# Longer transfer rows and fixed homes in one arena, in a fused linear attention and Soft-MoE kernel

## The chip, the cores and the metric

The kernel runs on one core of a Trainium2 chip. The metric is the device time of one execution in microseconds (us), lower is better. The engines are TensorE (PE, with its weight loads as PEld), VectorE (DVE), ScalarE (ACT), GpSimd (POOL) and SyncE (SP), which here does nothing but issue DMA transfers.

## What is computed

Linear attention for 8 batches, 8 heads, 576 tokens and 64 dimensions a head, then a Soft-MoE layer over all 4608 tokens with 8 experts of 4 slots each. All of it is float32. Cut to what matters, the reference is:

```python
kv  = einsum('bhsd,bhse->bhde', k, v)
o   = einsum('bhsd,bhde->bhse', q, kv)
x   = o / sqrt(mean(o*o, -1) + 1e-6) * g_norm          # -> (4608, 512)
logits = x @ phi                                       # (4608, 32)
d   = exp(logits - logits.max(0)); d /= d.sum(0) + 1e-9
slots = d.T @ x                                        # 4 rows for each expert
y[e] = relu(slots[e] @ w1[e]) @ w2[e]                  # w1 512x1024, w2 1024x512
c   = exp(logits - logits.max(1)); c /= c.sum(1) + 1e-9
out = c @ y                                            # (4608, 512)
```

## The kernel before, in words

The 4608 tokens are worked in 36 token tiles (T = 0 to 35) of 128 tokens; four batches' pairs share nine tiles. The kernel has two passes, separated by the softmax over all tokens.

*Pass 1.* For each batch b, `Kv.products` (L159) and `Kv.borders` (L174) make k^T v on PE from a main part (512 of the 576 tokens, two halves g = 0, 1 of two head pairs each) and a border part (the other 64 tokens). `Kv.slots` turns that into a block matrix `bd` that gives the attention output and its product with phi in one go. `products(T)` (L227, and L218 for the tile that two batches share) makes token tile T from q and `bd`. ACT and DVE square, reduce and evict it, GpSimd scales it to x (`xts`, 14 buffers) and to parts of the logits. Every six tiles make a group with a running maximum, an exponential, and a sum of weighted x (`group_sum`, L361). The tables `first` and `kv_steps` set between which tiles the steps of batch b's kv stand: three tiles ahead of its first use, one step a tile; batch 1's two halves and borders are worked at T = 2.

*Pass 2.* `expert_h(e)` (L573) multiplies the slots by w1, `expert_y(e, hf)` (L591) by half hf of the columns of w2. Experts 0 to 3 run as they come. For experts 4 to 7 all `expert_h` come first, then all first halves, `mix(0)`, and then the output of the first half of the columns, with the second halves of w2 worked in between: the output is made in three chunks k of 12 token tiles and two parts f, so six calls of `output` for hf = 0 and six for hf = 1. Experts 4 and 5, second half, are worked after call 1, expert 6 after call 2, expert 7 after call 3, then `mix(1)` and the rest. `output` (L619) multiplies on PE, evicts one half with ACT (L627) and the other with DVE (L629), and stores 768 KB (L630).

*Transfers.* All are issued by SP, in one list, in order. An input or weight tile of 1 MB has 8 KB in each of 128 partitions; border tiles (`kvr`, `qr`) have 2 KB. The 1 MB tiles and the output stages share a ring of 17 slots (`ring`, `NSLOT`), the border tiles five slots (`rest`). Half of one expert's w1 goes into four border slots (`SPLIT`), another expert's w1 into x buffers that are no longer needed (`IN_X`), in eight transfers of 2 KB rows. Each transfer waits until the one that is eight places earlier in the list has landed, since they share a completion semaphore; where its slot had a reader, it waits for that too.

Of the kernel before, what the change touches and what calls it, by code (L numbers as in the profile page):

```python
# [8 lines left out]
F32 = mybir.dt.float32  # L9
# [5 lines left out]
P = 128  # L15
# [16 lines left out]
SLOT = 2048  # L32
NSLOT = 17
SPLIT = (4, 0)
IN_X = ((5, 0), (5, 1))
NREST = 5
# [5 lines left out]
def soft_moe_linear_attention(ctx: ExitStack, tc: tile.TileContext, kv_in, kvr_in, q_in, qr_in, w1_in, w2_in, c_in, out):  # L42
# [5 lines left out]
    ring = ctx.enter_context(tc.tile_pool(name="ring", bufs=NSLOT))  # L48
    rest = ctx.enter_context(tc.tile_pool(name="rest", bufs=NREST))
    wk = ctx.enter_context(tc.tile_pool(name="wk", bufs=2))  # L50


    kv_sb, kvr_sb, q_sb, qr_sb, w1_sb, w2_sb = {}, {}, {}, {}, {}, {}

    def load_kv(b):
        kvr_sb[b] = rest.tile([P, 512], F32, tag="rest", name=f"kvr{b}")
        for g in range(2):
            kv_sb[b, g] = ring.tile([P, SLOT], F32, tag="ring", name=f"kv{b}_{g}")
            nc.sync.dma_start(kv_sb[b, g], kv_in[b, g])
            if b == 0 and g == 0:  # L60
                nc.sync.dma_start(cst, c_in)
            if g == (b > 0):
                nc.sync.dma_start(kvr_sb[b], kvr_in[b])

    def load_q(b):
        if b % 2:
            qr_sb[b // 2] = rest.tile([P, 2, NPAIR, 64], F32, tag="rest", name=f"qr{b // 2}")
            nc.sync.dma_start(qr_sb[b // 2], qr_in[b // 2])
        q_sb[b] = ring.tile([P, NPAIR, 512], F32, tag="ring", name=f"q{b}")
        nc.sync.dma_start(q_sb[b], q_in[b])  # L70

    def load_w1(e):
        for k in range(2):
            if (e, k) == SPLIT or (e, k) in IN_X:

                if (e, k) == SPLIT:
                    parts = [rest.tile([P, 512], F32, tag="rest", name=f"w1_{e}_{k}_{i}") for i in range(4)]
                else:
                    T = NT - GROUPS[-1] - 8 + 4 * IN_X.index((e, k))
                    parts = [xts[(T + i) % NX].rearrange("p j n -> p (j n)")[:, :512] for i in range(4)]  # L80
                for i, t in enumerate(parts):
                    nc.sync.dma_start(t, w1_in[e, k, :, i // 2, i % 2 * 512 : i % 2 * 512 + 512])
                w1_sb[e, k] = [[parts[2 * c + j // 2][:, j % 2 * 256 : j % 2 * 256 + 256] for j in range(4)] for c in range(2)]
                continue
            t = ring.tile([P, 2, FF], F32, tag="ring", name=f"w1_{e}_{k}")
            nc.sync.dma_start(t, w1_in[e, k])
            w1_sb[e, k] = [[t[:, c, j * 256 : (j + 1) * 256] for j in range(4)] for c in range(2)]

    def load_w2(e, hf):
        w2_sb[e, hf] = ring.tile([P, 8, 256], F32, tag="ring", name=f"w2_{e}_{hf}")  # L90
        nc.sync.dma_start(w2_sb[e, hf], w2_in[e, hf])
# [5 lines left out]
    for b in range(B):  # L97
        load_kv(b)
        load_q(b)
# [24 lines left out]
    xts = []  # L124
    for i in range(NX):
        t = const.tile([P, 4, 129], F32, name=f"x{i}")
        nc.gpsimd.memset(t[:, :, 128:129], 1.0)
        xts.append(t)
# [13 lines left out]
    class Kv:  # L142
# [10 lines left out]
        def products(self, r):  # L153
            g, w = divmod(r, 2)
            main = kv_sb[self.b, g].rearrange("p (r w c n) -> p r w c n", r=2, w=2, c=4)
# [11 lines left out]
        def borders(self, gs):  # L167

            half = kvr_sb[self.b].rearrange("p (g w n) -> p g w n", g=2, w=2)
            for g in gs:  # L170
                for i in range(2):
                    for w in range(2):
                        lo, at = 64 * i, 64 * w
                        nc.tensor.matmul(  # L174
                            self.pkv[lo : lo + 64, w, g],
                            lhsT=half[at : at + 64, g, 1, lo : lo + 64],
                            rhs=half[at : at + 64, g, 0, lo : lo + 64],
                            start=False,
                            stop=g == gs[-1],
                        )  # L180
# [30 lines left out]
    def products(T):  # L211
# [3 lines left out]
        for r in range(NPAIR):  # L215
            if t == 4:
                for i in range(2):
                    nc.tensor.matmul(  # L218
                        o[64 * i : 64 * i + 64, r, :192],
                        lhsT=qr_sb[g][:, i, r],  # L220
# [4 lines left out]
            else:  # L225
                i, at = (0, t * P) if t < 4 else (1, (t - 5) * P)
                nc.tensor.matmul(  # L227
                    o[:, r, :192], lhsT=q_sb[2 * g + i][:, r, at : at + P], rhs=bds[i][:, r], start=True, stop=True
# [193 lines left out]
    for T in range(NT - 2):  # L422
# [38 lines left out]
        for _ in range(min(2, len(todo_sums))):  # L461
            group_sum(*todo_sums.pop(0))

# [26 lines left out]
    for i in todo_sums:  # L490
        group_sum(*i)
    fill(LATE_FILL[0], home=ps.tile([P, 512], F32, tag="m", name="fill"), cols=512)
# [38 lines left out]
    LATE = 4  # L531
    for e in range(NE - LATE):
        load_w1(e)
        load_w2(e, 0)
        load_w2(e, 1)
    for e in range(NE - LATE, NE):
        load_w1(e)
    for hf in range(2):
        for e in range(NE - LATE, NE):
            load_w2(e, hf)  # L540

# [25 lines left out]

    def expert_h(e):
        ph = ps.tile([P, 2, 512], F32, tag="m", name=f"ph{e}")[:, 0, :256]
        for c in range(4):  # L570
            w1 = w1_sb[e, c // 2]
            for j in range(4):
# [3 lines left out]
                    rhs=w1[c % 2][j],  # L576
# [10 lines left out]
    def expert_y(e, hf):  # L587
        w2 = w2_sb[e, hf]
        for c in range(8):
# [4 lines left out]
                rhs=w2[:, c],  # L594
# [120 lines left out]
```

## Time and profile before

| what | value |
|---|---|
| median of 3 runs | 177.37 us (177.13 to 177.51) |
| profiled execution: span from its first to its last instruction | 175.2 us |
| profiled execution: its own whole time | not listed; the span and what lies around it, about 2 us by the median |
| PE busy | 150.1 us (86%) |
| DVE, ACT, POOL busy | 88.7, 87.0, 56.0 us |
| DMA queue of SP, share of 16 engines' span | 98.3% |
| read from HBM, written to HBM | 61.93 MB, 9.44 MB |
| mean rate over the span | 407 GB/s |

All times of a view count from the start of the span. In the busy digits of 40 slices, a digit is the busy share in tenths (9 is 90% or more). A row of the order of time gives start and duration in us, engine, line, operation, output <- input and a count; in brackets stands how long the engine sat idle before and what ended it. "SPq" is SP's queue: its duration is that of issuing, not of the transfer. A row of the waits gives who waited <- for whom: us in total, times, the longest. A row of the DMA issues gives the count, KB each, and the median us from issue to landing. A row of a stretch gives start:end and length, then for PE, PEld, DVE, ACT and POOL the busy us and in parentheses the instructions, then the granted clock, the share of the DMA engines and GB/s.

### The profile page before, as it was taken

To read this page: it belongs to the slowest core of one execution; us is meant where nothing else is said; L and a number is where in the kernel's file an instruction comes from. 1 tells how busy PE (TensorE), PEld (TensorE's weight loads), DVE (VectorE), ACT (ScalarE), POOL (GpSimd) and SP (SyncE) were. 2 spreads that over 40 slices of the span, in tenths; PEclk is the share of its full clock that TensorE was granted. 3 is DMA by queue.
4 is the path that set the end of the run, shared out by engine and by line. 5 is a ranking of instruction groups with operands and counts; after the bars stand their busy time and mean duration, and the time that the engine had idled before them with its cause. 6 is when DMAs were issued, how large, how long until landed. Compare 5 with 4: busy or idle time off the path is not lost.

```text
span 175.2 us, 4888 instructions
## 1 busy us (share of the span) xinstructions
PE 150.1 (86%) x2033; PEld 108.3 (62%) x2033; DVE 88.7 (51%) x180; ACT 87.0 (50%) x224; POOL 56.0 (32%) x78
## 2 busy tenths in 40 slices
PE   7677999999989899999999869889979988989600
PEld 5456878899779788888986754556636533343200
DVE  1122155666466665557654679625886205357600
ACT  2116386878948957869777751102312203336400
POOL 7000156666556566364666465000000000000000
PEclk9999999999999999999999999999999999999975
DMA  5999999999999999999999999999999999999995
GB/s 185 413 428 414 424 424 427 422 419 421 428 419 424 419 419 424 423 426 417 436 419 423 432 426 420 413 395 369 415 423 428 421 428 423 419 420 415 425 426 209
DMA packets 12982, 71.69 MB, mean 409 GB/s; under 512 B 1440, under 2 KB 1568, under 8 KB 6176
## 3 DMA queue, kind: packets, MB, share of 16 engines
q1 hardware_dynamic: 12960, 71.37, 98.3%
q8 instruction: 16, 0.26, 0.5%
q14 instruction: 6, 0.05, 0.1%
HBM read 61.93 MB, written 9.44 MB: 407 GB/s over the span
## 4 chain that ended last, share of the span: by engine, by line
PE 39%; DMA 27%; DVE 12%; ACT 10%; issue 3%; POOL 2%; SPq 2%; POOLq 0%; DVEq 0%
PE o L227 17%; DMA w<-in_w_dram 16%; DMA kv<-in_kv_dram 8%; PE kvp_kv L159 8%; PE po L619 4%; DMA out_dram<-st 3%; DVE logits L304 3%; DVE st L629 3%; PE pS L361 2%; DVE ms L250 2%; POOL part L299 2%; ACT bd L194 2%; PE o L218 2%; ACT sq L237 2%; PE ph L573 2%
## 5 line engine op out<-in xcount | busy, mean ns | idle before, releaser
L227 PE MATMUL o<-bd,q 128*128 128x192 f32 x256 | 49.3, 336 | 1.5 <-ACT x L245 0.6
L227 PEld LDWEIGHTS o<-bd,q 128*128 128x128 f32 x256 | 40.8, 190 | 4.7 <-ACT x L245 1.6
L277 POOL TENSOR_TENSOR x<-x,r 128x512 f32<-128x512 f32 x34 | 34.7, 1042 | 0.0
L299 POOL TENSOR_TENSOR part<-part,r 128x512 f32<-128x512 f32 x17 | 17.8, 1048 | 50.7 <-DVE r L268 50.7
L304 DVE TENSOR_REDUCE logits<-part 128x64 f32<-128x512 f32 (+1 forms) x19 | 19.2, 1013 | 16.1 <-POOL part L299 16.0
L250 DVE TENSOR_REDUCE ms<-sq 128x16 f32<-128x1024 f32 (+1 forms) x19 | 22.0, 1157 | 6.3 <-ACT sq L237 6.3
L237 ACT ACTIVATE sq<-o 128x512 f32<-128x512 f32 x36 | 21.4, 596 | 6.6 <-PE o L227 6.1
L245 ACT COPY x<-o 128x512 f32<-128x512 f32 x34 | 20.7, 608 | 0.0
L159 PE MATMUL kvp_kv<-kv 128*64 128x64 f32 x480 | 17.3, 225 | 2.4 <-DMA kv<-in_kv_dram 2.4
L159 PEld LDWEIGHTS kvp_kv<-kv 128*64 128x64 f32 x480 | 15.2, 138 | 5.4 <-DMA kv<-in_kv_dram 3.1
L627 ACT COPY st<-po 128x768 f32<-128x768 f32 x12 | 9.4, 800 | 16.7 <-PE po L619 16.6
L591 PE MATMUL pY<-w,x 128*32 128x256 f32 x256 | 16.0, 382 | 1.2 <-DVE x L585 1.2
L629 DVE COPY st<-po 128x768 f32<-128x768 f32 x12 | 11.3, 956 | 7.9 <-PE po L619 5.9
L619 PE MATMUL po<-logits,z 32*128 32x384 f32 x96 | 13.8, 528 | 1.6 <-DVE st L629 0.6
L573 PE MATMUL ph<-w,sTe 128*32 128x256 f32 x224 | 13.0, 379 | 0.3 <-DVE sTe L514 0.3
L591 PEld LDWEIGHTS pY<-w,x 128*32 128x32 f32 x256 | 7.6, 109 | 8.3 <-DVE x L585 1.9
L244 ACT COPY part<-o 128x256 f32<-128x256 f32 x34 | 12.6, 371 | 0.0
L361 PE MATMUL pS<-x,d 128*32 128x129 f32 x288 | 10.7, 276 | 2.1 <-ACT d L349 2.1
L258 ACT ACTIVATE r<-ms,eps 128x16 f32<-128x16 f32 x17 | 5.2, 308 | 12.7 <-DVE ms L250 12.6
L619 PEld LDWEIGHTS po<-logits,z 32*128 32x128 f32 x96 | 5.5, 183 | 9.0 <-ACT st L627 3.6
L266 DVE SCALAR_TENSOR_TENSOR r<-ms,r 128x16 f32<-128x16 f32 x17 | 3.0, 176 | 14.9 <-ACT r L259 14.9
L573 PEld LDWEIGHTS ph<-w,sTe 128*32 128x32 f32 x224 | 7.2, 110 | 5.2 <-DVE sTe L514 0.6
(90 smaller groups left out, 146.7 us busy)
## 6 DMA issues: line engine op xcount, KB each, us to landing
w<-in_w_dram SPq DMA_DIRECT2D x29, 1024.0 KB, 19.1
kv<-in_kv_dram SPq DMA_DIRECT2D x16, 1024.0 KB, 14.3
out_dram<-st SPq DMA_DIRECT2D x12, 768.0 KB, 6.4
q<-in_qt_dram SPq DMA_DIRECT2D x8, 1024.0 KB, 14.2
kvr<-in_kr_dram SPq DMA_DIRECT2D x8, 256.0 KB, 14.9
x<-in_w_dram SPq DMA_DIRECT2D x8, 256.0 KB, 6.9
qr<-in_qr_dram SPq DMA_DIRECT2D x4, 256.0 KB, 14.1
w<-in_w_dram SPq DMA_DIRECT2D x4, 256.0 KB, 15.2
```

What stands on the lines that cost most here:

```text
L159: nc.tensor.matmul(self.pkv[lo : lo + 64, w, g], lhsT=main[:, w, 1, c, lo : lo + 64], rhs=main[:, w, 0, c, lo : lo + 64], start=c == 0 and ...
L227: nc.tensor.matmul(o[:, r, :192], lhsT=q_sb[2 * g + i][:, r, at : at + P], rhs=bds[i][:, r], start=True, stop=True)
L237: nc.scalar.activation(sqs[s][:, T - starts[s]], o[:, :, 32:160], AF.Square, scale=0.125)
L245: nc.scalar.copy(xts[T % NX][:, :, :128], o[:, :, 32:160])
L250: nc.vector.tensor_reduce(out=mss[s], in_=sqs.pop(s).rearrange("p t j (w d) -> p (t j w) d", w=2), axis=AX.X, op=ALU.add)
L277: nc.gpsimd.tensor_tensor(out=x, in0=x, in1=r[:, i].rearrange("p (j w) -> p j w", w=2).unsqueeze(3).to_broadcast([P, 4, 2, D]), op=ALU.mult,)
L299: engine.tensor_tensor(out=part, in0=part, in1=rs_of[s].unsqueeze(3).to_broadcast([P, STAGES[s], H, NS]), op=ALU.mult)
L304: nc.vector.tensor_reduce(out=L[:, pos(starts[s]) : pos(starts[s]) + STAGES[s]], in_=parts.pop(s).rearrange("p t h n -> p t n h"), axis=AX ...
L573: nc.tensor.matmul(ph[32 * j : 32 * j + 32], lhsT=sTe[:, (4 * e + c) * NS : (4 * e + c + 1) * NS], rhs=w1[c % 2][j], start=c == 0, stop=c ...
L591: nc.tensor.matmul(pY[32 * j : 32 * j + 32, hf, :256], lhsT=hTs[e][:, c], rhs=w2[:, c], start=e == 0 and c < 4, stop=e == NE - 1 and c >= 4,)
L619: nc.tensor.matmul(po[:, u, : CT * NS].rearrange("p (g x) -> p g x", g=2), lhsT=z[lo : lo + 32, f * P : (f + 1) * P], rhs=cT[k][lo : lo + 32],
L629: nc.vector.tensor_copy(out=st[:, 2:4], in_=po[:, :, : CT * NS])
```

## The change

*Layout.* kv and its border rows of a batch become one array with rows of 18 KB per partition (4608 numbers: for each half g 2048 main and 256 border numbers). The q of two batches and their shared border become one array with rows of 18 KB. A whole w1 of an expert has rows of 16 KB. A w2 has 16 KB too: for experts 0 to 3 both halves of the columns; for experts 4 to 7 unit 4 holds the first halves of experts 4 and 5, unit 5 those of 6 and 7, unit 6 the second halves of 4 and 5, unit 7 those of 6 and 7. The first loads are cut: kv of batches 0 and 1 in two rows of 9 KB each, the first two q arrays in 8 and 10 KB.

*Homes.* In place of the two rings there is one arena of 160 KB per partition. A table gives each load its home in it in units of 1 KB; a home is reused when the readers of what lay there are done. w1 of expert 5 goes into the x buffers (now one tile, `xall`, turned by six tiles), w1 of expert 6 into two pieces. 15 of 16 KB that GpSimd had as DMA scratch are taken for the arena.

*Stores.* Chunk k = 0 is stored as before in two transfers with rows of 6 KB; for k = 1 and 2 the two parts f go in one transfer with rows of 12 KB, issued once both are evicted.

The work of PE, ACT, DVE and GpSimd keeps its order. The core of the diff:

```diff
-SLOT = 2048
-NSLOT = 17
-SPLIT = (4, 0)
-IN_X = ((5, 0), (5, 1))
-NREST = 5
+TOK = 4608
+UNIT = 4096
+KB = 256
+ARENA = 160 * KB
+LATE = 4
+KV_AT = (0, 36, 54, 90, 108, 0, 18, 36)
+Q_AT = (18, 72, 142, 54)
+W_AT = {("w1", 0): (72,), ("w2", 0): (88,), ("w1", 1): (104,), ("w2", 1): (120,), ("w1", 2): (136,), ("w2", 2): (0,), ("w1", 3): (16,), ("w2", 3): (32,), ("w1", 4): (48,), ("w1", 5): None, ("w1", 6): (64, 152), ("w1", 7): (72,), ("w2", 4): (88,), ("w2", 5): (104,), ("w2", 6): (120,), ("w2", 7): (136,)}
+SCRATCH = 1024
...
+    def place(at, n):
+        return arena[:, at * KB : at * KB + n]
...
+    load_kv(0, 0)
+    nc.sync.dma_start(cst, c_in)
+    load_kv(0, 1)
+    load_q(0, 0)
+    load_kv(1, 0)
+    load_kv(1, 1)
+    load_q(0, 1)
+    load_kv(2)
...
+    loads_behind = {
+        9: lambda: (load_kv(5), load_kv(6), load_q(3), load_kv(7)),
+        18: lambda: [load_w(k, e) for e in range(2) for k in ("w1", "w2")],
+        27: lambda: (load_w("w1", 2), load_w("w2", 2), load_w("w1", 3)),
+        31: lambda: load_w("w2", 3),
+    }
...
-        st = ring.tile([P, 4, CT * NS], F32, tag="ring", name=f"st{hf}_{k}_{f}")
+        at = 6 * ((hf * NCH + k) * 2 + f)
+        st = place(at, 4 * CT * NS).rearrange("p (a n) -> p a n", a=4)
...
-        nc.sync.dma_start(out[hf, k, f], st)
+        if k == 0:
+            nc.sync.dma_start(out[hf, k, :, f], place(at, 4 * CT * NS))
+        elif f == 1:
+            nc.sync.dma_start(out[hf, k].rearrange("p f n -> p (f n)"), place(at - 6, 8 * CT * NS))
...
-    nc = bacc.Bacc("TRN2", target_bir_lowering=False, num_devices=1)
+    nc = bacc.Bacc("TRN2", target_bir_lowering=False, num_devices=1, dynamic_dma_scratch_size=SCRATCH)
```

The calls of `load_w` for the later weights stand among the work that frees their homes: w1 of experts 4 to 6 behind the last sums of x, w1 of expert 7 behind `expert_h(1)`, w2 units 4 and 5 behind `expert_y` of experts 0 and 1, units 6 and 7 behind that of expert 3.

Two places of SP's list show what moves. At its start the kernel before issues these; `kv_0` and `kv_1` are the halves of a batch, `kvr` its border rows, and the last number is of float32 per partition.

```order
L59 DMA kv_0_71<-in_kv_dram 128x2048
L61 DMA cst<-in_cs_dram 128x129
L63 DMA kvr_70<-in_kr_dram 128x512
L59 DMA kv_1_75<-in_kv_dram 128x2048
L70 DMA q_77<-in_qt_dram 128x2048
L59 DMA kv_0_80<-in_kv_dram 128x2048
L59 DMA kv_1_82<-in_kv_dram 128x2048
L63 DMA kvr_79<-in_kr_dram 128x512
L68 DMA qr_85<-in_qr_dram 128x512
L70 DMA q_87<-in_qt_dram 128x2048
```

The border rows of batch 1 (`kvr_79`) are a transfer of their own behind its second half. The changed kernel issues at the same place, with all of it in the arena:

```order
L66 DMA arena<-in_kv_dram 128x2304
L105 DMA cst<-in_cs_dram 128x129
L66 DMA arena<-in_kv_dram 128x2304
L70 DMA arena<-in_qt_dram 128x2048
L66 DMA arena<-in_kv_dram 128x2304 x2
L70 DMA arena<-in_qt_dram 128x2560
L66 DMA arena<-in_kv_dram 128x4608
```

Each half of batches 0 and 1 now carries its own border rows, and from batch 2 on a batch is one transfer. At the end of SP's list the kernel before has the last weights and, of its twelve stores, the six of hf = 0 as follows (the name gives k, then f):

```order
L91 DMA w_6_1_1609<-in_w_dram 128x2048
L91 DMA w_7_1_1611<-in_w_dram 128x2048
L630 DMA out_dram<-st_0_0_1921 128x1536
L630 DMA out_dram<-st_0_1_1931 128x1536
L630 DMA out_dram<-st_1_0_1957 128x1536
L630 DMA out_dram<-st_1_1_1975 128x1536
L630 DMA out_dram<-st_2_0_1999 128x1536
L630 DMA out_dram<-st_2_1_2009 128x1536
```

There each part is stored on its own. The changed kernel has at the end:

```order
L95 DMA arena<-in_w_dram 128x2048 x2
L95 DMA arena<-in_w_dram 128x4096 x5
L652 DMA out_dram<-arena 128x1536 x2
L654 DMA out_dram<-arena 128x3072 x2
L652 DMA out_dram<-arena 128x1536 x2
L654 DMA out_dram<-arena 128x3072 x2
```

Of each hf, stores 3 and 4 became one and stores 5 and 6 became one; the whole list has 42 transfers where there were 90.

More of the change, by code (lines that the diff above doesn't have):

```diff
@@ L41, in soft_moe_linear_attention @@
 @with_exitstack
-def soft_moe_linear_attention(ctx: ExitStack, tc: tile.TileContext, kv_in, kvr_in, q_in, qr_in, w1_in, w2_in, c_in, out):
+def soft_moe_linear_attention(ctx: ExitStack, tc: tile.TileContext, kv_in, q_in, w1_in, w2_in, c_in, out):
     nc = tc.nc
     const = ctx.enter_context(tc.tile_pool(name="const", bufs=1))
-    ring = ctx.enter_context(tc.tile_pool(name="ring", bufs=NSLOT))
-    rest = ctx.enter_context(tc.tile_pool(name="rest", bufs=NREST))
     wk = ctx.enter_context(tc.tile_pool(name="wk", bufs=2))
[L53 to L91, printed above, removed]
@@ L95, in soft_moe_linear_attention, with load_kv, load_q, kv_main @@
     g2 = cst[:, 128:129]
-    for b in range(B):
-        load_kv(b)
-        load_q(b)
+    arena = const.tile([P, ARENA], F32, name="arena")
+    xall = const.tile([P, NX, 4, 129], F32, name="xall")
+    xflat = xall.rearrange("p i j n -> p (i j n)")
+    def place(at, n):
+        return arena[:, at * KB : at * KB + n]
+    def load_kv(b, g=None):
+        lo, hi = (0, TOK) if g is None else (2304 * g, 2304 * g + 2304)
+        nc.sync.dma_start(place(KV_AT[b], TOK)[:, lo:hi], kv_in[b, :, lo:hi])
+    def load_q(g, half=None):
+        lo, hi = {None: (0, TOK), 0: (0, 2048), 1: (2048, TOK)}[half]
+        nc.sync.dma_start(place(Q_AT[g], TOK)[:, lo:hi], q_in[g, :, lo:hi])
+    def kv_main(b, g):
+        return place(KV_AT[b], TOK)[:, g * 2304 : g * 2304 + 2048]
+    def kv_rest(b, g):
+        return place(KV_AT[b], TOK)[:, g * 2304 + 2048 : g * 2304 + 2304]
+    def q_main(b):
+        return place(Q_AT[b // 2], TOK)[:, b % 2 * 2048 : b % 2 * 2048 + 2048].rearrange("p (r n) -> p r n", r=NPAIR)
+    def q_rest(g):
+        return place(Q_AT[g], TOK)[:, 4096:].rearrange("p (i r n) -> p i r n", i=2, r=NPAIR)
+    def homes(kind, u):
+        at = W_AT[kind, u]
+        if at is None:
+            return [xflat[:, :UNIT]]
+        return [place(a, UNIT // len(at)) for a in at]
+    def load_w(kind, u):
+        parts = homes(kind, u)
+        n = UNIT // len(parts)
+        for i, t in enumerate(parts):
+            nc.sync.dma_start(t, (w1_in if kind == "w1" else w2_in)[u, :, i * n : i * n + n])
+    def w_block(kind, u, i):
+        parts = homes(kind, u)
+        n = UNIT // len(parts)
+        k, at = divmod(i * 256, n)
+        return parts[k][:, at : at + 256]
+    load_kv(0, 0)
[6 more added lines that the diff above has]
+    load_kv(2)
+    load_q(1, 0)
+    load_kv(3)
+    load_q(1, 1)
+    load_kv(4)
+    load_q(2)
+    loads_behind = {
[4 more added lines that the diff above has]
+    }
     nc.scalar.preload_act_table_set("natural_log_exp_and_others")
@@ L123, in soft_moe_linear_attention @@
         nc.gpsimd.memset(bds[i], 0.0)
[L124 to L128, printed above, removed]
+    nc.gpsimd.memset(xall[:, :, :, 128:129], 1.0)
+    xts = [xall[:, (i + 6) % NX] for i in range(NX)]
     L = const.tile([P, NT + len(GROUPS) + 1, NS], F32, name="logits")
@@ L167, in borders @@
         def borders(self, gs):
-            half = kvr_sb[self.b].rearrange("p (g w n) -> p g w n", g=2, w=2)
             for g in gs:
+                half = kv_rest(self.b, g).rearrange("p (w n) -> p w n", w=2)
                 for i in range(2):
@@ L491, in soft_moe_linear_attention @@
         group_sum(*i)
+    for e in range(4, 7):
+        load_w("w1", e)
     fill(LATE_FILL[0], home=ps.tile([P, 512], F32, tag="m", name="fill"), cols=512)
@@ L701 @@
     arrays = {
-        "in_kv_dram": kv,
-        "in_kr_dram": kr,
+        "in_kv_dram": kv.reshape(B, P, TOK),
         "in_qt_dram": qm,
-        "in_qr_dram": qr,
         "in_w1_dram": np.ascontiguousarray(w1),
```

71 lines of the change are left out of this document (39 added, 32 removed).

## The prediction

> **What bounds the kernel now.** I read the profile's page first: the span, the busy digits and the DMA queues.
>
> ```profile
> span 175.2 us, 4888 instructions
> ...
> DMA  5999999999999999999999999999999999999995
> ...
> DMA packets 12982, 71.69 MB, mean 409 GB/s; under 512 B 1440, under 2 KB 1568, under 8 KB 6176
> ...
> q1 hardware_dynamic: 12960, 71.37, 98.3%
> ```
>
> The one queue of SP keeps the 16 DMA engines busy for 98.3% of the span. That looks like a kernel which ends when its bytes have been moved, so that whatever makes a byte cheaper makes it faster. The packets are the rows of the transfers and one mark per engine and transfer (90 transfers x 16 = 1440 under 512 B).
>
> Two things have to be asked before that is believed: who waits for a load, and what feeds the queue at the end. The waits by engine answer the first; only these rows name a load as what a compute engine on PE waited for.
>
> ```profile
> PEld kvp_kv L159 <- DMA kv<-in_kv_dram: 3.1, 3, 1.3
> PE kvp_kv L159 <- DMA kv<-in_kv_dram: 2.4, 3, 1.1
> PE kvp_o L159 <- DMA kv<-in_kv_dram: 1.0, 1, 1.0
> PEld pY L591 <- DMA w<-in_w_dram: 0.5, 1, 0.5
> ```
>
> The kv waits belong to the first batches, before 18 us, as PE's order of time shows:
>
> ```profile
> 15.61 1.15 PE L159 MATMUL kvp_kv<-kv 128*64 128x64 f32 x32 [0.49 <-DMA kv<-in_kv_dram]
> 17.91 1.15 PE L159 MATMUL kvp_kv<-kv 128*64 128x64 f32 x32 [1.15 <-DMA kv<-in_kv_dram]
> 18.99 0.46 PE L174 MATMUL kvp_kv<-kvr 64*64 64x64 f32 x16
> ```
>
> From there to the end the sum of load waits is 0.5 us: the arithmetic is a second chain, as long as the transfers, and loads run ahead of it. The second question is answered by the stores. These are issue times on SP (start, us) of stores 1, 5 and 6, and of the last:
>
> ```profile
> 147.25 0.35 SPq L630 DMA_DIRECT2D out_dram<-st  x1
> 156.73 0.33 SPq L630 DMA_DIRECT2D out_dram<-st  x1
> 158.48 1.20 SPq L630 DMA_DIRECT2D out_dram<-st  x2
> 166.06 0.35 SPq L630 DMA_DIRECT2D out_dram<-st  x1
> ```
>
> and these the DMA issues, in the windows of stores 1, 5, 6 and 12, with the time from issue to landing at the end of the line:
>
> ```profile
> out_dram<-st SPq DMA_DIRECT2D x1, 768.0 KB, 6.7
> out_dram<-st SPq DMA_DIRECT2D x1, 768.0 KB, 4.6
> out_dram<-st SPq DMA_DIRECT2D x1, 768.0 KB, 4.7
> out_dram<-st SPq DMA_DIRECT2D x1, 768.0 KB, 8.2
> ```
>
> Store 1 lands at 153.95 and store 12 at 174.26, one every (174.26 - 153.95) / 11 = 1.85 us. Store 5 lands only 4.6 us after its issue, 1.85 of them its own bytes. So at 156.7 us the queue is nearly empty: 4.6 less 1.85 leaves 2.75 us for what an issue always takes and for everything still ahead of it. The engines then live on what ACT and DVE evict. This place decides the case.
>
> **What fewer transfers save.** The change moves the same bytes in 42 transfers instead of 90, 128 rows each. The cost of a transfer beside its bytes is read from SP's order of time, where each issue waits for an earlier landing: two 1 MB transfers, and four in the pace of 256 KB ones.
>
> ```profile
> 79.04 2.75 SPq L91 DMA_DIRECT2D w<-in_w_dram  x2
> 118.04 2.34 SPq L86 DMA_DIRECT2D w<-in_w_dram  x4
> ```
>
> An issue lasts 0.33 us, so landings are 2.75 - 0.33 = 2.42 us apart for 1 MB, and (2.34 - 0.33) / 3 = 0.67 for 256 KB; a 768 KB store took 1.85. From the stores, 256 KB cost (1.85 - 0.67) / 2 = 0.59 us, and 0.67 - 0.59 = 0.08 us is left per transfer; the 1 MB rows give 0.58 and 0.09. The spacing is read to some 0.03 us, so I take 0.08 with bounds of 0.05 and 0.11: 48 x 0.08 = 3.8 us less work for the queue (2.4 to 5.3), if a row of 18 KB stays one packet. The trace has no such row of SP's.
>
> The last weight transfer landed at 152.0:
>
> ```profile
> 132.44 0.33 SPq L91 DMA_DIRECT2D w<-in_w_dram  x1
> w<-in_w_dram SPq DMA_DIRECT2D x1, 1024.0 KB, 19.6
> ```
>
> Ahead of it and with it stand 78 transfers now and 34 afterwards, so the weights are in at 152.0 - 44 x 0.08 = 148.5 us.
>
> **Homes.** Each load now waits until the last reader of its home is done. I walked the list with 8 x 0.59 + 0.08 = 4.80 us per 2 MB unit. The last q landed at 71.6, which becomes 71.6 - 20 x 0.08 = 70.0.
>
> ```profile
> 57.40 0.33 SPq L70 DMA_DIRECT2D q<-in_qt_dram  x1
> q<-in_qt_dram SPq DMA_DIRECT2D x1, 1024.0 KB, 14.2
> 79.94 1.47 PE L227 MATMUL o<-bd,q 128*128 128x192 f32 x8
> 101.02 1.55 PE L227 MATMUL o<-bd,q 128*128 128x192 f32 x8
> 115.92 3.66 PE L573 MATMUL ph<-w,sTe 128*32 128x256 f32 x64 [0.28 <-DVE sTe L514]
> ```
>
> w1 of expert 2 is fifth, due on the engines at 70.0 + 4 x 4.80 = 89.2, and its home is free after token tile 26 (81.4). w1 of expert 4 is ninth, due at 108.4, free after tile 35 (102.6). w1 of expert 7 is due at 122.9, and its home is free after expert 0's products, half of the last row (117.8). The margins are 5 us and more, and up to 8 transfers may be in flight, so I count the waits for homes at nothing. Once a margin is gone, each us costs a us of queue.
>
> **The start.** The second half of batch 1's kv now brings its border rows along. In the kernel before, PE started on that half at 17.91, the moment it landed; the border rows came one 256 KB transfer later:
>
> ```profile
> 4.13 0.45 SPq L63 DMA_DIRECT2D kvr<-in_kr_dram  x1
> kvr<-in_kr_dram SPq DMA_DIRECT2D x1, 256.0 KB, 14.4
> ```
>
> at 18.53. Afterwards everything up to there lands together, two transfers sooner by count: 18.53 - 0.16 = 18.4, so PE starts 0.5 us later. It then works with hardly a pause until the sums (97% busy from 30 to 60 us), so nothing absorbs the delay: +0.5 us on all evictions behind it (bounds 0 and 0.67).
>
> ```profile
> 30.00:60.00 30.00, 28.93 (x393) 24.83 (x388) 18.64 (x38) 24.34 (x69) 18.30 (x18) 1.00 1.02 422
> ```
>
> **The end.** Stores of chunks 1 and 2 are now paired: the pair of chunk 2, first half, is issued when store 6 was, at 158.48 + 0.5 = 158.98. What stands ahead of it is done by then: the weights at 148.5, 1.85 us for each of two stores, and the pair of chunk 1, which can be issued only with store 4. So the engines stand still, and an issue into an empty queue has to be priced. The trace has one, the first of the kernel, and the engines' first and last moments (40 slices of 0.7 to 2.3 us, and of 173 to 175.2):
>
> ```profile
> 0.74 0.37 SPq L59 DMA_DIRECT2D kv<-in_kv_dram  x1
> kv<-in_kv_dram SPq DMA_DIRECT2D x1, 1024.0 KB, 4.8
> DMA  0000000000000000000000000090000090009099
> DMA  5705570275222000000000000000000000000000
> ```
>
> The first packet starts in slice 27, at 1.74, 1.0 us after the issue; at the end the last packet is gone by 173.9 and the landing counts at 174.26, 0.4 later. That is 1.4 us at least. The whole first transfer took 4.8 us, of which 2.42 are bytes: 2.4 us at most, with a cold start in it. I take 1.7, nearer to the lower end, since a store isn't the first access of the run.
>
> By the Trainium skill, DMA: Bandwidth & Descriptors, section Anatomy of one DMA — SWDGE (gpsimd) path, a transfer has a fixed part of about 2.0 us; it is fitted on GpSimd's path, the trace's bounds hold it, and by it the end would come 0.3 us later than by my 1.7.
>
> Behind that issue stand 3 pairs and 2 single stores, 6 MB: 24 x 0.59 + 5 x 0.08 = 14.5 us, all evicted faster than they are moved (store 12 was issued 7.6 us after store 6). The last landing is 158.98 + 1.7 + 14.5 = 175.2, against 174.26: +0.9 us. The 3.8 us saved are spent in the idle time before that pair, for nothing on PE, ACT or DVE comes earlier. The span of 175.2 becomes 176.1; the median of the runs shown, 177.37, lies 2.1 above the span, and I add the difference to it: **178.3 us**.
>
> The rest has one answer: fewer waits on PE and one fill of the ones column instead of 14 are off the path; all DMA issues on the page are SP's, so the smaller scratch of GpSimd costs nothing.
>
> **Rivals.**
>
> *The bytes decide after all.* Evictions come earlier than I think, or long rows save more, and the queue never runs dry: 173.6 to 175.0 by the 2.4 to 3.8 us, some part of it being likelier than all. For it speaks 98.3%; against it the 4.6 us of store 5, which leave at most 1.3 us to win even with single stores (4.6 - 1.85 - 1.4). Chance 0.13. The Trainium skill, same page, section Rules for kernel authors, speaks for large transfers, and its section Bandwidth shows 341 GB/s at 1 MB and 425 at 16 MB; by that the gain would be far more, but the windows below show that 1 MB transfers in a row already run at 425, so it bears on transfers that stand alone.
>
> ```profile
> 136.00:147.00 11.00, 9.70 (x131) 4.50 (x123) 2.52 (x5) 1.78 (x4) 0.00 (x0) 1.00 1.01 425
> ```
>
> *It comes out even.* The 0.5 us at the start is absorbed and the empty queue costs 1.4: 158.48 + 1.4 + 14.5 = 174.4, +0.1, 177.5 us. Chance 0.15.
>
> *Weights come late.* Long rows run slower, or a home is freed late. It decides once the last w2 unit lands after PE's turn for expert 6, second half:
>
> ```profile
> 150.58 1.07 PE L591 MATMUL pY<-w,x 128*32 128x256 f32 x16
> ```
>
> that is after 151.1; each us beyond delays all later evictions by a us. At 3% less rate the 62 MB of loads take 4.4 us more, 152.9 instead of 148.5: +1.8 on top, 180.1 us. Chance 0.10.
>
> **How the numbers follow.** The forecast keeps 0.62. Its own bounds are 158.48 + 0 + 1.4 + 14.5 = 174.4 and 158.48 + 0.67 + 2.4 + 14.5 = 176.0, so 177.5 to 179.1. The range for 8 in 10 reaches a little into the rivals on both sides: 177.2 to 179.4. A measurement here can tell some 0.2%, 0.35 us, from no change. Slower: the forecast but for 0.05 at its lower end (0.57), and the late weights: 0.67. Same: 0.05, the even case and a piece of the first rival: 0.21. Faster: 0.12.
>
> **What would show it.** Right: the page's DMA digits drop below 9 in the slices near 153 to 160 us, the last weights land near 148.5, PE has no longer wait for w, the pair of chunk 2 is issued near 159.0 and the last landing follows 16 us later. The start is right if PE's second half of batch 1 begins near 18.4. Wrong: digits of 9 through to the end (the first rival), PE waiting for w from 120 us on (the third), or the pair landing sooner than 1.4 us and its bytes after the issue.

## The result, and the profile after

The changed kernel takes **179.32 us** in the median of 4 runs (179.29 to 179.40), against 177.25 (177.09 to 177.51) for the kernel before: a ratio of 1.0117, with an interval of 1.0103 to 1.0132. It is 2.1 us slower. The forecast was 178.3 us, with a range of 177.2 to 179.4. The profiled execution took 179.34 us, its span 177.5. A few executions of some kernels below ran at a lower granted clock and took 3% longer or more; they enter no ratio.

The page of the changed kernel, its span, digits, rates and queue, is read first:

```profile
span 177.5 us, 4779 instructions
...
DMA  6999999999999999999999999999999998679994
GB/s 197 416 431 422 451 400 438 422 432 432 411 445 411 438 415 432 421 427 417 436 421 430 417 432 428 432 406 427 434 423 428 414 428 350 259 314 400 433 415 169
DMA packets 6069, 71.68 MB, mean 404 GB/s; under 512 B 672, under 2 KB 800, under 8 KB 1312
...
q1 hardware_dynamic: 6048, 71.37, 95.6%
```

The change did what it says: less than half as many packets carry the same bytes, and a row stayed one packet at every length (42 transfers of 128 rows and 16 marks are the 6048 packets). Yet the queue is now busy for 95.6% of a longer span. Behind the first slice the digits stay at 9 up to slice 33, counted from 1; slices 34 to 36 show 8, 6 and 7. A slice is 177.5 / 40 = 4.44 us, so these three lie between 146.4 and 159.7 us, and the rate falls to 259 GB/s in the middle one, from 150.9 to 155.3. Two stretches, in the kernel before:

```profile
152.00:155.00 3.00, 2.45 (x30) 1.03 (x26) 1.59 (x3) 0.80 (x1) 0.00 (x0) 1.00 1.01 422
158.00:160.00 2.00, 1.64 (x14) 0.66 (x12) 1.79 (x3) 1.04 (x2) 0.00 (x0) 1.00 1.01 415
```

and in the changed one:

```profile
152.00:155.00 3.00, 2.45 (x34) 1.03 (x26) 1.66 (x3) 0.86 (x2) 0.00 (x0) 1.00 0.37 154
158.00:160.00 2.00, 1.64 (x18) 0.52 (x13) 1.82 (x2) 0.80 (x1) 0.00 (x0) 1.00 0.43 174
```

So there are two holes where the queue was full before. The first lies ahead of the pair of chunk 1, the second ahead of the pair of chunk 2; behind the second the queue is as good as full, so it is the one that sets the end. (The 8 of slice 34 is the tail of the weights: the 16 DMA engines are done with the last unit between 147.44 and 151.15, each at its own time.)

What SP issues around the holes, in its order of time (start, duration of the issue): the last two weight units, the pair of chunk 1 and that of chunk 2 of the first half of the columns, and the very last store.

```profile
125.18 0.80 SPq L95 DMA_DIRECT2D arena<-in_w_dram  x2
154.24 0.33 SPq L654 DMA_DIRECT2D out_dram<-arena  x1
159.10 0.33 SPq L654 DMA_DIRECT2D out_dram<-arena  x1
166.67 0.33 SPq L654 DMA_DIRECT2D out_dram<-arena  x1
```

And these are the DMA issues at those places, with us from issue to landing at the end: the last weight unit, the three pairs, and the packets by queue in the stretch from 158 to 161 us.

```profile
arena<-in_w_dram SPq DMA_DIRECT2D x1, 2048.0 KB, 25.6
...
out_dram<-arena SPq DMA_DIRECT2D x1, 1536.0 KB, 5.7
...
q1 hardware_dynamic: 78, 0.76, 63.2%
q8 instruction: 1, 0.02, 1.9%
...
out_dram<-arena SPq DMA_DIRECT2D x1, 1536.0 KB, 6.5
...
out_dram<-arena SPq DMA_DIRECT2D x1, 1536.0 KB, 9.8
```

The weights are in at 151.15. The pair of chunk 1 is issued at 154.24 and landed at 159.97; the pair of chunk 2 is issued at 159.10, when next to nothing is left ahead of it, and lands 6.5 us later, at 165.56. From 158 to 161 us the queue is busy for only 63.2% of what it could be, and one packet of the instruction queue (q8) falls into that stretch. The last landing is 166.67 + 9.8 = 176.47 us, against 174.26 before: the 2.2 us by which the span is longer are all there at the end.

The starts and idle times on PE, in its order of time: the second half of batch 1's kv, the first expert, and the first half of the columns of expert 6.

```profile
18.27 1.15 PE L181 MATMUL kvp_kv<-arena 128*64 128x64 f32 x32 [1.01 <-DMA arena<-in_kv_dram]
...
116.28 3.66 PE L593 MATMUL ph<-arena,sTe 128*32 128x256 f32 x64 [0.28 <-DVE sTe L540]
...
141.51 1.07 PE L611 MATMUL pY<-arena,xall 128*32 128x256 f32 x16 [0.16 <-DMA arena<-in_w_dram]
```

PE begins the half of batch 1 at 18.27 (17.91 before) and the first expert at 116.28 (115.92 before): the 0.36 us lost at the start travel through the kernel unchanged. Expert 6 then has to wait for its weights, which it didn't before.

### The profile page after: what moved, and what is told of

Read it like the earlier page. It is cut to its first block, busy times and chain, and to the rows that moved or that the text cites. A ratio compares the mean times of both kernels' runs of the same rounds, so it can differ in the third digit from the quotient of the medians.

```text
span 177.5 us, 4779 instructions
## 1 busy us (share of the span) xinstructions
PE 151.5 (85%) x2033; PEld 109.5 (62%) x2033; DVE 88.8 (50%) x180; ACT 87.0 (49%) x224; POOL 55.7 (31%) x65
## 3 DMA queue, kind: packets, MB, share of 16 engines
q1 hardware_dynamic: 6048, 71.37, 95.6%
## 4 chain that ended last, share of the span: by engine, by line
PE 46%; DMA 19%; DVE 12%; ACT 10%; issue 3%; POOL 2%; SPq 2%; POOLq 0%; DVEq 0%
PE o L249 17%; DMA arena<-in_w_dram 11%; DMA arena<-in_kv_dram 8%; PE kvp_kv L181 8%; PE po L640 6%; PE pY L611 4%; DVE logits L326 3%; DVE arena L650 2%; PE pS L383 2%; PE ph L593 2%; DVE ms L272 2%; POOL part L321 2%; ACT bd L216 2%; PE o L240 2%; ACT sq L259 2%
## 5 line engine op out<-in xcount | busy, mean ns | idle before, releaser
L249 PE MATMUL o<-bd,arena 128*128 128x192 f32 x256 | 49.3, 336 | 1.7 <-ACT xall L267 0.6
L249 PEld LDWEIGHTS o<-bd,arena 128*128 128x128 f32 x256 | 40.8, 190 | 4.8 <-ACT xall L267 1.6
L299 POOL TENSOR_TENSOR xall<-xall,r 128x512 f32<-128x512 f32 x34 | 34.8, 1044 | 0.0
L267 ACT COPY xall<-o 128x512 f32<-128x512 f32 x34 | 20.6, 607 | 0.0
L181 PE MATMUL kvp_kv<-arena 128*64 128x64 f32 x480 | 17.3, 225 | 2.2 <-DMA arena<-in_kv_dram 2.2
L181 PEld LDWEIGHTS kvp_kv<-arena 128*64 128x64 f32 x480 | 15.2, 138 | 5.3 <-DMA arena<-in_kv_dram 3.1
L611 PE MATMUL pY<-arena,xall 128*32 128x256 f32 x256 | 16.0, 382 | 1.4 <-DVE xall L605 1.2
L650 DVE COPY arena<-po 128x768 f32<-128x768 f32 x12 | 11.3, 956 | 7.9 <-PE po L640 7.9
L593 PE MATMUL ph<-arena,sTe 128*32 128x256 f32 x224 | 13.0, 379 | 0.3 <-DVE sTe L540 0.3
L383 PE MATMUL pS<-xall,d 128*32 128x129 f32 x288 | 10.7, 276 | 2.1 <-ACT d L371 2.1
```

The costliest lines, as they stand in the source:

```text
L181: nc.tensor.matmul(self.pkv[lo : lo + 64, w, g], lhsT=main[:, w, 1, c, lo : lo + 64], rhs=main[:, w, 0, c, lo : lo + 64], start=c == 0 and ...
L249: nc.tensor.matmul(o[:, r, :192], lhsT=q_main(2 * g + i)[:, r, at : at + P], rhs=bds[i][:, r], start=True, stop=True)
L267: nc.scalar.copy(xts[T % NX][:, :, :128], o[:, :, 32:160])
L299: nc.gpsimd.tensor_tensor(out=x, in0=x, in1=r[:, i].rearrange("p (j w) -> p j w", w=2).unsqueeze(3).to_broadcast([P, 4, 2, D]), op=ALU.mult,)
L593: nc.tensor.matmul(ph[32 * j : 32 * j + 32], lhsT=sTe[:, (4 * e + c) * NS : (4 * e + c + 1) * NS], rhs=w_block("w1", e, 4 * c + j), start= ...
L611: nc.tensor.matmul(pY[32 * j : 32 * j + 32, hf, :256], lhsT=hTs[e][:, c], rhs=w_block("w2", u, at + c), start=e == 0 and c < 4, stop=e == ...
```

## The experiments

The main theory was that of the prediction: the loss is the idle queue in front of the pairs, because a pair holds back the bytes of its first part until the second is evicted. The first rival was that long rows move more slowly, or arrive too late, since the weights landed at 151.15 instead of the forecast 148.5. A third suspect came up when the rows were compared with the program's layout: in the changed kernel the arena begins at byte 1696 of each partition, 160 bytes beyond a multiple of 256, while the ring's slots before began on such multiples.

**All stores single.** The changed kernel with 12 stores of 768 KB.

```diff
-        if k == 0:
-            nc.sync.dma_start(out[hf, k, :, f], place(at, 4 * CT * NS))
-        elif f == 1:
-            nc.sync.dma_start(out[hf, k].rearrange("p f n -> p (f n)"), place(at - 6, 8 * CT * NS))
+        nc.sync.dma_start(out[hf, k, :, f], place(at, 4 * CT * NS))
```

> The changed kernel with all twelve stores issued singly again (rows of 6 KB, each as soon as it is evicted); the loads, the arena and the homes stay. Theory A (the pairs of the first half of the columns hold bytes back while the DMA engines run dry, and the engines never get that time back): no dry stretch of any length, store 5 issued near 157.4 us of the span and the engines busy from there, so last landing near 157.4 + 1.4 + 8 x 1.85 = 173.6 instead of 176.5, and 176.3 to 177.0 us, below the kernel before (177.25) by what the loads save. Theory B (the long-row loads arrive late and the whole end shifts, the pairs cost little): 179.0 us or more, within 0.4 of the changed kernel.

Measured: 177.45 us (176.71 to 178.15), ratio to the kernel before 1.0027 (1.0007 to 1.0046). The digits of its page:

```profile
DMA  5999999999999999999999999999999998989995
```

Store 5 and the last store, in SP's order of time:

```profile
157.35 0.33 SPq L651 DMA_DIRECT2D out_dram<-arena  x1
...
166.68 0.36 SPq L651 DMA_DIRECT2D out_dram<-arena  x1
```

and in the DMA issues, with the packets by queue from 156 to 159 us:

```profile
q1 hardware_dynamic: 166, 0.90, 75.5%
q8 instruction: 1, 0.02, 2.3%
...
out_dram<-arena SPq DMA_DIRECT2D x1, 768.0 KB, 4.3
...
out_dram<-arena SPq DMA_DIRECT2D x1, 768.0 KB, 7.8
```

Most of the 2.1 us is back, 1.9 by the medians and 1.6 by the two ratios, with long rows, homes and the start left as they are. So the pairs cost the time, and long rows don't. But the time is above the 176.3 to 177.0 us that were expected, and still a little above the kernel before. Store 5 is issued 0.62 us later than there (157.35 against 156.73), and still the queue runs dry ahead of it: 75.5% from 156 to 159 us, with an instruction fetch (q8) in that stretch too.

**Pairs only in the second half of the columns.**

```diff
-        if k == 0:
+        if k == 0 or hf == 0:
```

> The changed kernel with pairs kept only in the second half of the columns, where the queue is long; the first six stores are single. Theory A: as with all stores single, 176.2 to 177.0 us; four transfers fewer move it by at most 0.2. Theory B: within 0.4 of the changed kernel (179.3).

Measured: 177.35 us (176.96 to 177.73), ratio 1.0016 (1.0002 to 1.0029), the last landing at 174.10. It is again above the expected 176.2 to 177.0, but level with all stores single: the two pairs that cost 1.6 to 1.9 us in the first half cost nothing in the second, where stores are queued behind one another. What hurts is the place of a pair, and the place is where the queue has nothing else.

**Weights in rows of 8 KB.** The changed kernel, pairs included, with each weight unit loaded in two transfers.

```diff
-        n = UNIT // len(parts)
-        for i, t in enumerate(parts):
+        for i in range(2):
+            n = UNIT // 2
+            parts = homes(kind, u)
+            t = parts[i] if len(parts) == 2 else parts[0][:, i * n : i * n + n]
```

> The changed kernel with each 16 KB-row weight unit loaded by two transfers with 8 KB rows; homes, order and stores stay, so that only the row length and the number of transfers change (17 more). If a long row saves what the prediction reckoned (0.08 us per transfer): last weights land 16 x 0.08 = 1.3 us later (152.4 instead of 151.15), PE waits for them 1.2 us and the time is 180.3 to 180.7 us. If a row of 16 KB costs as much as two of 8 KB (second theory on the size of the saving): last weights within 0.3 us of 151.15 and 179.1 to 179.6 us.

Measured: 178.98 us (178.86 to 179.24), ratio 1.0115 (1.0099 to 1.0132). The last weights land at 152.03, 0.9 later than in the changed kernel, between the two expectations, and the time stays where it was. The length of the weights' rows is not what the loss hangs on. (The halves also bring the weights of two experts one by one, so this run speaks of both together.)

**The kernel before, with stores held back.** This is the other side of the first experiment: short rows, the ring, 90 transfers, and only the first part of chunks 1 and 2 kept until the second is ready. A first attempt did nothing:

```diff
-        nc.sync.dma_start(out[hf, k, f], st)
+        held_st[f] = st
+        for h in (f,) if k == 0 else (0, 1) if f == 1 else ():
+            nc.sync.dma_start(out[hf, k, h], held_st[h])
```

> The kernel before, with short rows, ring and all, where stores 3 and 5 of each half of the columns are held back and issued together with stores 4 and 6; same 90 transfers. Theory A: holding alone costs the time. Store 5 is issued at 158.5 instead of 156.7, into an empty queue; from there 1.4 to 2.8 us and 8 x 1.85 = 14.8 us to the last landing, 174.7 to 176.1 instead of 174.3: 177.7 to 179.1 us. Theory B: holding costs nothing, 177.1 to 177.5 us.

Measured: 176.96 us (176.74 to 177.47), ratio 0.9999 (0.9987 to 1.0012). It tells nothing of the theories: SP's list kept its order, each store waited only for its own evictions, and stores 3 and 5 were issued at 151.64 and 156.60, no later than before. What holds a store back is the one ahead of it in the list. So the second attempt turned the two round, the later part first:

```diff
-        for h in (f,) if k == 0 else (0, 1) if f == 1 else ():
+        for h in (f,) if k == 0 else (1, 0) if f == 1 else ():
```

> The kernel before, with stores 3 and 4 (and 5 and 6) of each half of the columns in exchanged order in SP's list, so that the earlier part really waits behind the later one; nothing else changes. Theory A (held bytes meet a dry queue): store 5 goes out at 158.4 instead of 156.6; the last landing is 158.4 + 1.4 to 2.4 + 8 x 1.85 = 174.6 to 175.6 instead of 174.0, so 177.6 to 178.6 us against 177.05. Theory B (the pairs cost nothing, the cost of the change lies in its loads): 176.9 to 177.2 us.

Measured: 178.95 us (178.5 to 179.45), ratio 1.011 (1.0083 to 1.0137). Its page:

```profile
span 177.2 us, 4884 instructions
...
DMA  5999999999999999999999999999999999989994
```

SP's order of time, chunk 1's two stores and the first of chunk 2's:

```profile
154.01 0.81 SPq L634 DMA_DIRECT2D out_dram<-st  x2
...
158.87 0.33 SPq L634 DMA_DIRECT2D out_dram<-st  x1
```

and the DMA issue of the latter:

```profile
out_dram<-st SPq DMA_DIRECT2D x1, 768.0 KB, 4.4
```

Not one transfer is larger than before, and the loss is that of the changed kernel (1.011 against 1.0117), 0.35 us more than the most that was expected. Store 5, issued at 156.73 before, now stands behind one that goes out at 158.87 and needs 4.4 us to land, of which 1.85 are its bytes. The digits hardly show it: one 8 in the place of a 9.

**The arena on a multiple of 256 bytes.** The changed kernel with pairs; the arena moves to the front, behind a pad, so that it begins at byte 1280 instead of 1696.

```diff
+    pad = const.tile([P, 32], F32, name="pad")
+    arena = const.tile([P, ARENA], F32, name="arena")
+    xall = const.tile([P, NX, 4, 129], F32, name="xall")
+    nc.gpsimd.memset(pad, 0.0)
...
-    arena = const.tile([P, ARENA], F32, name="arena")
-    xall = const.tile([P, NX, 4, 129], F32, name="xall")
```

> The changed kernel with the arena moved from byte 1696 to byte 1280 of each partition, so that every home begins at a multiple of 256 bytes, as the slots of the ring in the kernel before did; pairs kept. Theory C (rows that begin off such a boundary cost some 6 ns more each, and this ate the saving of the longer rows): 2 MB units land 4.84 to 4.86 us apart instead of 4.90, the last weights at 149.5 to 150.0 instead of 151.15; the time moves little by theory A, 178.6 to 179.3 us, since the end hangs on the evictions. Theory D (place doesn't matter): weights at 151.0 to 151.3 us.

Measured: 179.16 us (178.96 to 179.97), ratio 1.013 (1.0101 to 1.0159). Its digits:

```profile
span 177.3 us, 4780 instructions
...
DMA  6999999999999999999999999999999997579993
```

SP's order of time, the last two weight units and the pair of chunk 2:

```profile
125.29 0.80 SPq L97 DMA_DIRECT2D arena<-in_w_dram  x2
...
158.94 0.33 SPq L656 DMA_DIRECT2D out_dram<-arena  x1
```

and its DMA issues, the last weight unit and that pair:

```profile
arena<-in_w_dram SPq DMA_DIRECT2D x1, 2048.0 KB, 24.2
...
out_dram<-arena SPq DMA_DIRECT2D x1, 1536.0 KB, 6.4
```

The weights are in at 149.88, 1.3 us sooner than at 151.15, by where their rows begin (in the next run, with the same loads, at 150.20). And the time is the same: the holes are deeper (7, 5, 7 in the place of 8, 6, 7), the pair is issued at 158.94 instead of 159.10, and from there on everything takes as long as before.

**Aligned and single.** Both edits together, the first and the one above.

> Aligned arena and all stores single. Theory A: 1.4 us or more of earlier weights buy nothing, because store 5 still waits for its evictions: 176.8 to 177.5 us, no more than 0.3 below the kernel before. If the queue's bytes decide: 174.9 to 176.0 us.

Measured: 176.68 us (175.99 to 177.08), ratio 0.9975 (0.9957 to 0.9992). This beats both kernels: the one before by 0.25%, within that interval, and the changed one by its whole loss and a little more. It is about what was expected if the evictions decide (176.8 to 177.5), and above the 174.9 to 176.0 if the queue's bytes did. Store 5 in SP's order of time:

```profile
157.09 0.33 SPq L653 DMA_DIRECT2D out_dram<-arena  x1
```

and in its DMA issues, with the time to its landing:

```profile
out_dram<-arena SPq DMA_DIRECT2D x1, 768.0 KB, 4.1
```

The rest of the gain is small for the reason already seen: 44 transfers fewer than before end the loads sooner, and the queue still waits for an eviction, at 157 us.

**Without the idle products.** Between the first halves of experts 4 to 7, PE works three products of zeros that nobody reads (`PACED`, 0.50 us at each place in the trace). With loads done sooner they might be what delays the evictions, so they were taken away, first from the aligned kernel with single stores, then from the kernel before.

```diff
-PACED = 3
+PACED = 0
```

> As the one with aligned arena and single stores, and without the nine filler matmuls among the first halves of experts 4 to 7, which paced PE to the loads of the kernel before (1.3 us of PE). Theory A: all evictions come up to 1.3 us earlier, now that the loads allow it, and the time falls by as much, 175.6 to 176.4 us, under both kernels. If PE then waits for the weights instead: 176.8 to 177.3 us.

Measured: 177.47 us (176.86 to 178.01), ratio 1.0016 (0.9999 to 1.0034). It was a miss. Store 5 is issued earlier, as hoped, as SP's order of time has it:

```profile
156.40 0.33 SPq L653 DMA_DIRECT2D out_dram<-arena  x1
```

But it lands no earlier, by its DMA issues, here with the packet of q8 from 156 to 162 us:

```profile
q8 instruction: 1, 0.02, 1.0%
...
out_dram<-arena SPq DMA_DIRECT2D x1, 768.0 KB, 5.8
```

The first of the 16 DMA engines is done with this store at 159.46, fifteen by 159.61, the last at 162.16. By the list of packets fifteen begin the store's rows at 157.24 to 157.38; the sixteenth's first row begins at 159.45, when a packet of the instruction queue (q8), 16 KB of the program itself, has run from 158.53 to 159.46. In the profiled run the 0.7 us won by the issue are lost to that one engine.

> The kernel before without the nine filler matmuls. Its weights land too late to let PE run ahead (expert 7's first half at 142.19 us, worked at 142.37), so by theory A PE waits where it ran fillers: 176.9 to 177.4 us, no change against 177.05. If the fillers by themselves cost time: 175.7 to 176.3 us.

Measured: 177.22 to 178.78 us in five runs, ratio 1.0052 (1.0027 to 1.0078), span of the profiled run 175.4. PE now waits for a weight where the idle products stood, as its order of time shows:

```profile
142.09 1.07 PE L591 MATMUL pY<-w,x 128*32 128x256 f32 x16 [1.41 <-DMA w<-in_w_dram]
```

It came out a little slower than expected. In the profiled run itself the span is hardly longer; why the timed runs are is left open.

**Another order of the last experts.** From the aligned kernel with single stores: expert 7's second half and `mix(1)` are worked later, so that stores 5 and 6 come earlier.

```diff
-    late = {1: (0, 1), 2: (2,), 3: (3,)}
+    late = {1: (0, 1), 2: (2,), 4: (3,)}
...
-        if i == 3:
+        if i == 5:
```

> Aligned arena, single stores, and the outputs of the first half of the columns made without a pause: expert 7's second half is worked between outputs 5 and 6 instead of between 4 and 5, and the y and z of the second half are made after output 6 instead of after output 4. The same work in another order. Theory A (the end hangs on when store 5 and its followers are evicted, and the earlier loads are worth time only if evictions keep the queue fed): store 5 is issued near 155.9 instead of 157.1, store 6 near 157.8 instead of 158.8, the queue is not dry behind the last weights (150.2) but for an instruction fetch, last landing 172.4 to 173.5 instead of 174.1: 175.0 to 176.2 us. If store 7, whose evictions come no earlier, then sets the end: 176.4 to 177.0 us.

Measured: 177.9 us (176.57 to 178.67, 12 runs), ratio 1.004 (1.0015 to 1.0065): a miss. The digits of its page:

```profile
DMA  5999999999999999999999999999999997897996
```

Store 7 in SP's order of time:

```profile
161.36 0.33 SPq L653 DMA_DIRECT2D out_dram<-arena  x1
```

and its DMA issue:

```profile
out_dram<-arena SPq DMA_DIRECT2D x1, 768.0 KB, 3.2
```

Stores 5 and 6 are issued at 155.73 and 157.63 and land within 3.6 and 3.5 us, but store 7 now comes at 161.36, and the second hole (7 in slice 37) is its own. The hole has been moved, not closed. The times fall into two groups, five runs of 176.6 to 176.9 us and seven of 177.9 to 178.7. The profiled run is the shortest of the twelve, so these rows tell nothing of the longer group, which stays open.

**Loads alone, in rows of 2 to 32 KB.** Arithmetic is left out; the kernel loads weights one behind the other into an arena, and stores some of what it has loaded. In the first, the arena begins 128 bytes beyond a multiple of 256 (byte 1152), in the second on one (1280). Each ran once, on two chips.

```diff
+    for kb in (8, 2, 4, 6, 8, 9, 10, 12, 14, 16, 18, 24, 32):
+        for _ in range(max(1, round(48 / kb))):
+            load(kb * KB)
```

> Loads alone: stages of about 6 MB each with rows of 8, 2, 4, 6, 8, 9, 10, 12, 14, 16, 18, 24 and 32 KB per partition, contiguous in HBM, then six stores with rows of 6 KB and three with rows of 12 KB; all arithmetic is left out. The prediction's model (0.59 us per 256 KB and 0.08 us per transfer whatever the row): time per 256 KB falls steadily, 0.67 at 2 KB rows, 0.61 at 8 KB, 0.60 at 16 KB and 0.595 at 32 KB. Second theory (a row over 8 KB costs a second fixed part, as if it were cut): a step back up between 8 and 9 KB rows, and no gain from 8 to 16 KB.

> The loads alone again, with their area moved from byte 1152 to byte 1280 of each partition, a multiple of 256; all arithmetic is left out. Theory C: every transfer is 0.03 to 0.05 us shorter at any row length (1 MB 2.44 instead of 2.48, 2304 KB 5.45 instead of 5.50). Theory D: unchanged within 0.01 us.

Two stretches of the first, with rows of 2 KB (20 to 32 us) and of 8 KB (70 to 78 us); the columns behind the length are POOL's busy time, the clock, the share of the DMA engines and GB/s:

```profile
20.00:32.00 12.00, 0.00 (x0) 1.00 1.06 387
70.00:78.00 8.00, 0.00 (x0) 1.00 1.02 424
```

and the same of the second:

```profile
20.00:32.00 12.00, 0.00 (x0) 1.00 1.05 406
70.00:78.00 8.00, 0.00 (x0) 1.00 1.01 428
```

In us per transfer, read from the steps between landings:

| row | 2 KB | 4 KB | 8 KB | 12 KB | 16 KB | 18 KB | 32 KB |
|---|---|---|---|---|---|---|---|
| 128 bytes beyond | 0.677 | 1.279 | 2.485 | 3.692 | 4.901 | 5.496 | 9.712 |
| on a multiple | 0.646 | 1.248 | 2.464 | 3.658 | 4.838 | 5.454 | 9.671 |

Each 2 KB more per partition costs about 0.60 us from 2 KB rows to 32 KB rows, so the theory of a further fixed part for rows over 8 KB falls. A transfer's own fixed part is small: on a multiple, (4.838 - 0.646) / 7 = 0.599 us for 256 KB leave 0.047 us for a transfer. Beginning beside the multiple costs 0.02 to 0.06 us a transfer at every length.

## Why the prediction was right, step by step

The side, the place and the mechanism came as forecast: an idle queue ahead of the pair of chunk 2, behind which everything follows at the queue's pace. The time is another matter. 179.32 us lies beyond the forecast's own bounds of 177.5 to 179.1, and inside the range only because that had been stretched towards the rivals. That is luck, for what filled the gap was no rival's mechanism but, for the most part, one slow DMA engine, as told below. Of the sum, each term:

*The reading of store 5.* The prediction took its 4.6 us to mean that the queue was nearly empty in the kernel before. But store 4, issued at 153.62, landed at 159.46, and store 5 at 161.33: 1.87 us later, a store's bytes and no more. The stretches above show the queue at 101% there. The kernel before lost no time at this place; its evictions came just in time for its transfers, so that both set its end. What the forecast needed is less, and held: evictions come no earlier, so that time saved on the queue becomes idle time.

*What fewer transfers save.* The forecast had the weights in at 148.5, 3.5 us sooner; it was 0.9 (152.0 to 151.15). Two things were wrong. The 0.08 us per transfer was too much: loads alone show 0.047, and 44 times that is 2.1 us, about what the aligned arena shows (152.0 - 149.88, and 152.0 - 150.20 in its second run). The other 1.0 to 1.3 us went to rows that begin beside a multiple of 256 bytes, which the prediction left out. None of this moved the time: with the weights 1.3 us sooner or 0.9 later, the kernel with pairs takes 179.16 and 178.98 us. The first rival, that the bytes decide, needs exactly this to be otherwise.

*Homes.* Nothing, as forecast: the digits are 9 up to slice 33.

*The start.* +0.5 us was forecast, and the starts of PE show +0.36. (PE's row from 30 to 60 us gives 28.93 of 30.00, which is 96% and not 97%.) But a second delay was missed. The w2 of experts 6 and 7 is now one unit of 2 MB, and PE reaches expert 6 before all of it is in. These are the waits for loads of the changed kernel, but for kv:

```profile
PEld pY L611 <- DMA arena<-in_w_dram: 0.6, 1, 0.6
PE pY L611 <- DMA arena<-in_w_dram: 0.2, 1, 0.2
```

The prediction said that PE would have no longer wait for w; it has a short one, and expert 6 starts 0.58 us later than before instead of 0.36 (141.51 against 140.93). Both delays together put the pair's issue at 159.10, 0.62 behind store 6 of the kernel before; 158.98 was forecast. Here two errors nearly cancel, which is luck too.

*The issue into an empty queue.* This is the step that was mis-sized: 1.7 us beside the bytes, with bounds of 1.4 and 2.4, where 2.8 was measured (6.46 us less the 6 x 0.599 + 0.047 = 3.64 that 1536 KB take). Issue and landing hide what happened in between. The first DMA engine is done with the pair at 164.03 and fifteen of the sixteen by 164.18, 5.08 us after the issue, which is 1.4 beside the bytes: the lower bound. The last is done at 165.56. The trace does not name a packet's engine, but the packets in their order of time tell it here: fifteen begin the pair's rows at 159.93 to 160.08 and need 0.47 us for a row; the sixteenth has the packet of q8 (159.47 to 160.40), 16 KB of instructions, begins its first row at 160.39 and needs 1.51 us for it. A landing counts when all 16 engines are done, so the slowest of them sets it; and with the queue full from then on, most of the lag stays to the end. There fifteen engines are done at 175.39 and the last at 176.47. In the kernel before, where a q8 packet ran from 157.67 to 158.63 beside a full queue, the last two are done at 174.22 and 174.25. So of the 2.2 us some 1.1 is the wait of all the engines, and 1.1 the lag of one, which the prediction had not in its sum. The run with stores turned round has both as well: 175.18 and 176.20.

*What stands behind it.* After the pair came 4.5 MB: 18 x 0.59 + 4 x 0.08 = 10.9 us by the forecast's terms, 176.47 - 165.56 = 10.91 measured. It fits in part by chance: the fifteen engines took 175.39 - 164.18 = 11.21, and the late one made up 0.3 of its lag.

The sum was 158.98 + 1.7 + 14.5 = 175.2, and 176.47 came: 0.12 from the issue, 1.1 from the empty queue, nothing from the rest. What lies around the span was 179.34 - 177.5 = 1.84 us rather than the 2.1 that were added, which took back some 0.3; hence 179.3 rather than 178.3.

*The rivals.* "The bytes decide after all" fell, for the queue did run dry, and "it comes out even" as well, by 2.1 us. Late weights were right only in kind: its sign, PE waiting for weights behind 120 us, showed in those 0.2 us, but they never made PE wait for expert 6's second half, which starts at 151.20, 0.05 after the unit landed. A little more, and that rival would have added its price.

*What the loss is, then.* Holding back alone gives 1.011 with nothing else changed, and undoing the pairs brings 1.6 to 1.9 of the 2.1 us back. That half of the loss came by the one engine that fetched instructions in the hole is read from the profiled runs alone; no run moved the fetch on purpose, so it is not shown that this half would go with the fetch elsewhere. In the run with another order of the experts a q8 packet (160.49 to 161.47) fell into a hole before any row of the next store, and no engine lagged: store 7 was done at 164.59 on fifteen engines and at 164.60 on the last. By the Trainium skill, DMA: Bandwidth & Descriptors, section Rules for kernel authors, transfers should be 1 MiB or more for the most bandwidth. Here stores of 1.5 MB lose to stores of 0.75 MB by about 1%, since 0.047 us for a transfer saved is nothing against 1.85 us of bytes that wait.

## What to carry to other kernels

A queue that is busy for 98% of the span need not be the only bound: find the place where it is fed just in time, for there a saving on the queue is lost, and a larger transfer is a later one. Merge stores where others are queued ahead of them, and leave them small where each is issued as soon as it is evicted. To price an issue into an empty queue, look at the first and the last of the 16 engines, and not at the landing alone.

## What the runs showed of the hardware

*Where a row begins matters.* Loads into rows that begin 128 bytes beside a multiple of 256 run at 387 GB/s, those on a multiple at 406, with 2 KB rows; with 16 KB rows it is 4.90 against 4.84 us. The table's gap is 0.02 to 0.06 us for 128 rows. The weights of this kernel came 1.0 and 1.3 us sooner, in two runs, with the arena at byte 1280 instead of 1696. The Trainium skill, DMA: Bandwidth & Descriptors, section How a descriptor splits into AXI transactions, has extra beats for a descriptor that doesn't start on a multiple of 256 bytes, and tells this of reads. These runs show a price where the written side begins beside such a multiple; what it consists of they don't show.

*The program is fetched through the same engines.* The profile has 16 packets of 16 KB in the instruction queue, on before as on after. What most of them cost is open. At 159.5 us in the changed kernel and at 158.5 us in the aligned kernel without idle products, one made a landing 1.5 and 2.7 us later than the quickest engine's, and the last landing of the run 1.1 and 2.3 us later than the other fifteen engines'.

*A small hole is hard to see.* In the kernel before with its stores turned round, 1.9 us were lost at digits of 9 but for one 8, since a slice is 4.4 us and a digit shows its mean. Nor does the store's own row show it, for its 4.4 us to a landing are no more than the 4.6 of store 5 in the kernel before, where nothing was lost. The step from the landing ahead of it shows it: 159.72 to 163.32, 3.60 us for a store of 1.85, against 1.87 there.
